# Row maxima go by one transfer from an SBUF strip into the query stacks, and the instruction order is planned anew with other delays

## The chip, the core and the metric

The kernel runs on one core of one Trainium2 chip. The metric is the device time of one execution in microseconds; lower is better. Kernel times are medians of several runs, and the profile is one further execution with the hardware profiler on. The engines are TensorE (PE; PEld is its weight load), VectorE (DVE), ScalarE (ACT), GpSimd (POOL) and SyncE (SP), which issues nearly all DMA transfers. Each engine takes its instructions strictly in program order and waits on semaphores for the others.

## The reference

A sequence of 2048 tokens of width 640 goes through two attentions of 32 heads of 20 columns, and a sigmoid gate per token mixes them (in short):

```python
g = sigmoid((x * gate_w).sum(-1, keepdims=True))
return g * A(x) + (1 - g) * B(x)

# A: four segments of 512 tokens
logits = q_s @ k_s.T * scale + mask              # causal within the segment
o = sig(beta) * (phi(q_s) @ M) / (phi(q_s) @ z + 1e-6) + (1 - sig(beta)) * softmax(logits) @ v_s
M = M + phi(k_s).T @ v_s;  z = z + phi(k_s).sum()  # phi(t) = t + 1 if t > 0 else exp(t)
# B: causal, window of 256 tokens
softmax(where(mask, q @ k.T * scale, -1e9)) @ v
# each with its own projections wq, wk, wv (wqkv) and wo
```

All is float32. The projections run in TensorE's float32r format; to keep the precision, their operands are split into a high half and a low half (the rest), and three products are added.

## The kernel before

The work is cut into 16 stages T (four segments times four groups of 16 heads; `head(T)` gives the group, in the order 0, 2, 1, 3, and the segment; groups 0 and 1 are attention A, 2 and 3 are B) and each stage into 4 units, so 64 units u of one segment, four heads at a time and two row halves r of TensorE. A unit takes about 15 us. Per stage TensorE makes the q and k projections (`gemm2`, L547) and the v projection (`v_mm`, L688); their weights and x chunks are split into halves by ScalarE (`copy`, L485) and by `split_l` (L501), which GpSimd or VectorE runs. A tiny copy named tick (L485 or L487) hands a PSUM bank from one row half to the other. The projections are stored to DRAM (`qk_store`, L591 and L593; `phi_store`, L615) and read back, rearranged, into one of four query stacks `qks` in SBUF (`stack_read`, L761, and for attention B L766 for q and L764 for k). So unit u + 4 uses the stack of unit u again.

Attention needs every row's maximum before the exponentials:

1. `max_mm` (L790): TensorE multiplies q and k, 16 matmuls a unit, into a PSUM bank per row half; `max_red` (L800): VectorE adds the mask and takes the row maximum, 16 times a unit, into `mx`, 128 x 16.
2. `max_high`, `max_low` (L804 ScalarE, L808 GpSimd) split the maxima into two halves in `mrs`, 128 x 32; `max_turn` (L812, VectorE) transposes it in blocks of 32 x 32 into `mt`, 128 x 32.
3. `max_store` (L816, SyncE) writes `mt` to DRAM (`dmx`), in an order that makes rows of 512 queries; `max_rows` (L820, SyncE), twice a unit, reads two rows of 1024 back into partitions 60 and 61 (and 124 and 125) of the query stack.
4. `st_mm` (L844): TensorE multiplies k and q again, with the two extra rows, so that the maximum is taken off inside the matmul; ScalarE takes the exponential into `P` (`st_exp`, L851), GpSimd cuts the diagonal (L857, L860), and TensorE multiplies by v (`av_mm`, L876). VectorE and GpSimd transpose, divide and transpose back (L947, L956, L974, L979, L983, L987), and the result goes by DRAM to the output projection (L547 with `ohl`, at the very end L539).

The order of instructions is not written out by hand. Each step is given to `Plan.add` with a due time in units, the engine (or two engines, "pool|dve", of which the planner takes one), a length and what it reads and writes. `Plan.order` then plays the engines: at each step it takes, among the items whose inputs are ready, the one that can start first (within TO or TP), by the shifted due time, and puts it at the end of its engine's program. The lags between engines in that play are FROM_PE, TO_PE (XP) and OTHER (XO), a transfer lands after its issue, its packets' time and DM. Due times come from constants: a stack is read at u - RD, the maxima stand at u - MT + i MQ, the steps of the maxima at u - MS; a table SHIFT moves each kind of step by an amount for each stage. DP is a handicap of VectorE where it and another engine could take an item.

Of the kernel before, what the change touches and what calls it, by code (L numbers as in the profile page):

```python
# [20 lines left out]
DH = 20  # L21
S = 2048
L = 512
# [15 lines left out]
NXS, NWS, NH, CAP = 4, 2, 1, 7  # L39
TP, TO, GP = 0.003, 0.0247, -0.9848  # L40
SW, SX, EV, WX, WS = 0.0838, 1.1218, 0.4057, 2, 1
AHEAD, RD, PACE = 6.0079, 2.1812, 3.8108
TA, TB, TC, WL = 3.9765, 0.2, 0.6, 0.0166
P0, MA, DP, NF, NR = 4.4219, 0.7417, 0.1294, 1, 1
MQ = 0.059
MT, MS = 1.677, 0.6472
WARM = 26
LM, LR, LA, AT = 0.6542, 1.1233, 0.108, 0.1204
DM, DS, SV, XP, XO, XS = 1.2, 0.35, 1.2, 0.2, 0.15, 0.04
# [3 lines left out]
ML, MN, QF, XT, OC, PL = -0.4052, -0.1569, 0.789, 0.0334, 0.1092, -0.6407  # L53
FE = -17
BACK, BULK, FT, FL = 3.3992, -1.1875, 1.0, 63
EPS = 1e-6
KINDS = dict(v_mm="v", max_mm="x", st_mm="s", tiled_mm="t", mem_add="a", split_h="h", split_l="l", m_high="e", m_low="e", v_out="e",
# [3 lines left out]
    a=(0.906, 0.762, 0.711, 0.288, -0.209, -3.157, -0.759, -0.444, 2.687, -1.073, -0.036, -1.619, 0.786, -0.987, 0.501, -1.076, 1.313, -0.983),  # L61
    c=(0.731, -0.093, -0.385, -0.167, -0.708, 0.703, 0.113, -0.061, 0.619, -0.11, -1.531, 0.072, -0.295, 0.055, -0.214, 0.043, -0.116, 0.411),
    d=(0.746, 0.239, 0.185, -0.082, 0.39, -0.063, 0.049, 0.317, -0.528, -0.276, -0.057, 0.559, -0.263, -1.344, -0.501, -0.266, 0.361, 1.353),
    e=(-4.249, 1.705, -0.128, 1.795, -1.311, 0.375, 0.842, -0.859, -0.461, 0.272, 0.494, -0.544, -0.178, -0.287, 2.233, 0.044, -2.89, 1.8),
    h=(3.212, -2.663, 1.644, 0.274, -0.301, 0.013, 0.501, -0.114, -0.071, -0.293, 0.303, 0.463, -0.151, 0.762, -0.002, -0.347, 0.662, -0.328),
    k=(-1.744, -0.243, 1.033, 0.232, -1.993, -0.368, -0.02, -0.301, -1.273, 0.311, -0.255, -1.133, -1.234, -0.63, 0.61, -0.279, -0.896, -0.594),
    l=(-0.219, -0.343, 4.432, 0.781, -0.987, 1.191, 0.933, -0.293, -0.21, 1.28, -0.466, 0.015, 1.949, -0.379, 0.201, 0.427, -0.789, -0.258),
    m=(-0.194, -1.25, -0.559, 0.371, -0.176, -0.004, 0.425, -0.115, 0.656, -0.29, -0.044, 0.247, 0.485, 0.245, 0.058, 0.06, 1.813, -2.594),
    o=(0.447, 0.881, 0.107, 0.382, 0.356, 0.191, -0.067, -0.696, 0.079, 0.169, 0.62, 0.011, -0.183, 0.133, 0.283, 0.535, -0.544, -0.683),
    p=(-1.445, -1.34, 2.498, -0.474, 0.624, 2.786, -1.141, -0.742, -0.084, -1.343, 0.092, -0.609, 0.968, 2.279, 0.395, 2.302, 0.043, -1.228),  # L70
    q=(-2.546, 0.691, 1.246, -0.428, 0.638, -0.221, -0.402, 0.036, -1.863, -1.785, 0.296, 0.473, 0.706, 0.742, -2.897, 0.134, 0.48, 1.045),
    r=(-1.009, -0.59, -0.055, 0.287, -0.49, -0.014, -0.236, 0.411, -0.328, 0.404, -0.154, -0.199, 0.678, -0.837, 1.105, -0.417, 0.238, 0.648),
    s=(-0.013, 0.309, -0.873, -0.733, 0.119, 0.011, 0.192, -0.467, -0.129, 0.092, -0.213, -1.611, -0.06, -0.193, -0.209, -0.054, -0.151, -0.401),
# [298 lines left out]
def attention(ctx, tc, const, dram, xt, wqk, wv, wo, beta, o_dram, out):  # L372
# [94 lines left out]
    def pair(w):  # L467

        return max(0.108, w * 0.000449 + 0.001)
# [333 lines left out]
    def max_high(u):  # L803
        nc.scalar.activation(mrs[u % 2][:, 0:16], B["M", u], AF.Copy)  # L804
# [483 lines left out]
```

## Time and profile before

| | |
|---|---|
| Median of 3 runs | 1002.24 us (997.16 to 1002.91) |
| Profiled execution, own time | 998.83 us |
| its span, first to last instruction | 997.1 us |
| mean granted TensorE clock | 0.994 |
| TensorE busy | 980.8 us, 98% |
| VectorE busy | 759.8 us, 76%, 2638 instructions |
| ScalarE busy | 666.9 us, 67%, 1601 instructions |
| GpSimd busy | 635.1 us, 64%, 862 instructions |
| DMA queue | 246.62 MB, 79.1% of 16 engines' span |

In the page and the views, a row such as "L790 <- DMA qks<-dkb: 3.9, 1, 3.9" of the waits is: who waited, for whom, us in all, times, longest. A row of the groups ends in busy us, mean ns of one, and the idle time just before them with what ended it. A row of the chain or of a timeline starts with its start and its length in us. A row of the windows has the stretch, its length, then the busy time of PE, PEld, DVE, ACT and POOL, the granted clock, the DMA share and GB/s. SPq is SyncE's queue, where a row's length is that of issuing a transfer. TensorE's busy share says that some matmul was under way; two row halves run at once, so a busy TensorE may still run one half alone.

### The profile page before, as it was taken

Reading aid. Unit: us, or ns where it says so; the run is one execution under the profiler, and the core shown is the slowest. Engines: PE = TensorE matmul, PEld = TensorE weight load, DVE = VectorE, ACT = ScalarE, POOL = GpSimd, SP = SyncE. Lnnn points to the kernel's source line nnn. Section 1 sums busy time; section 2 is a strip of 40 time slices with the busy share of each in tenths; the row PEclk is TensorE's granted clock in tenths of the full one; section 3 lists DMA queues with packets and bytes.
Section 4 is the critical chain, followed back from the end, with each engine's and each line's share of the span. In section 5 each row is a group of like instructions: output and inputs, shape, how many; then the busy total and the mean of one; then the engine's idle time right before and its main releaser. Section 6 shows DMA issues by size and latency. Waiting matters only on the chain.

```text
span 997.1 us, 30570 instructions
## 1 busy us (share of the span) xinstructions
PE 980.8 (98%) x11295; PEld 823.4 (83%) x11295; DVE 759.8 (76%) x2638; ACT 666.9 (67%) x1601; POOL 635.1 (64%) x862
## 2 busy tenths in 40 slices
PE   8999999999999899999999999999999999999998
PEld 7998888788878798888988898798888888877776
DVE  3279888888888586887867888679777886788944
ACT  4437767878577585776867676586677766755671
POOL 4335466847575496766966478585786666955650
PEclk9999999999999899999999999999999999999999
DMA  8899898889987879789798787969977898486433
GB/s 279 275 307 280 277 275 287 241 271 277 285 253 221 280 220 298 244 262 288 237 272 277 232 273 218 272 195 311 316 224 232 242 299 270 146 262 204 169 97 101
DMA packets 158037, 248.57 MB, mean 249 GB/s; under 512 B 52032, under 2 KB 68288, under 8 KB 157888
## 3 DMA queue, kind: packets, MB, share of 16 engines
q1 hardware_dynamic: 157888, 246.62, 79.1%
q8 instruction: 89, 1.46, 0.6%
q14 instruction: 60, 0.49, 0.2%
HBM read 150.88 MB, written 95.68 MB: 247 GB/s over the span
## 4 chain that ended last, share of the span: by engine, by line
PE 87%; DMA 5%; DVE 4%; SPq 1%; ACT 1%; POOL 1%; issue 1%; DVEq 0%; ACTq 0%
PE bank L547 40%; PE bank L688 15%; PE bank L876 14%; PE bank L790 8%; PE bank L844 8%; DMA wst<-wqk 3%; DVE bank L800 2%; PE bank L539 1%; PE bank L903 1%; DMA qks<-dkb 1%; DMA wvs<-wv 1%; PE bank L923 1%; DMA out<-ys 1%; POOL w L501 1%; DVE ys L1027 0%
## 5 line engine op out<-in xcount | busy, mean ns | idle before, releaser
L851 ACT ACTIVATE P<-bank 128x512 f32<-128x512 f32 (+2 forms) x768 | 382.1, 552 | 114.9 <-PE bank L844 73.3
L547 PE MATMUL bank<-xhl,w 64*128 64x512 f32 x2400 | 454.4, 400 | 0.5 <-DVE xhl L501 0.4
L547 PEld LDWEIGHTS bank<-xhl,w 64*128 64x128 f32 x2400 | 326.3, 186 | 12.7 <-DVE xhl L501 1.1
L790 PE MATMUL bank<-qks 60*128 60x384 f32 (+3 forms) x1024 | 302.0, 334 | 5.8 <-DMA qks<-dkb 3.9
L688 PE MATMUL bank<-wv,xhl 64*128 64x320 f32 (+1 forms) x1920 | 290.5, 317 | 1.9 <-ACT wv L485 1.3
L800 DVE CUSTOM_DVE_ANT_0 bank<-bank,mask_b 128x384 f32<-128x384 f32 (+2 forms) x512 | 259.9, 555 | 30.4 <-PE bank L790 25.0
L800 DVE CUSTOM_DVE_ANT_0 bank<-bank,mask_a 128x256 f32<-128x256 f32 (+3 forms) x512 | 239.9, 513 | 40.1 <-PE bank L790 29.2
L844 PE MATMUL bank<-qks 62*128 62x384 f32 (+3 forms) x1216 | 263.6, 303 | 2.6 <-ACT P L851 1.4
L688 PEld LDWEIGHTS bank<-wv,xhl 64*128 64x128 f32 x1920 | 247.2, 188 | 6.3 <-issue 2.1
L547 PE MATMUL bank<-ohl,w 64*128 64x512 f32 x1050 | 226.3, 400 | 0.4 <-DVE tick_dve L487 0.2
L501 POOL TENSOR_TENSOR w<-wst,w 128x640 fp32r<-128x640 f32 x109 | 170.4, 1565 | 82.6 <-ACT w L485 74.5
L857 POOL TENSOR_SCALAR_AFFINE_SELECT P<-P 128x512 f32<-128x512 f32 x256 | 161.5, 638 | 89.3 <-ACT P L851 73.6
L844 PEld LDWEIGHTS bank<-qks 62*128 62x128 f32 x1216 | 197.8, 186 | 19.7 <-issue 4.5
L790 PEld LDWEIGHTS bank<-qks 60*128 60x128 f32 x1024 | 177.3, 185 | 24.3 <-issue 11.9
L876 PE MATMUL bank<-P,vau 128*32 128x384 f32 (+3 forms) x2432 | 159.9, 407 | 0.5 <-DVE mx L800 0.2
L547 PEld LDWEIGHTS bank<-ohl,w 64*128 64x128 f32 x1050 | 153.4, 185 | 6.7 <-issue 0.8
L800 DVE DVE_READ_ACCUMULATOR2_ANT mx<- 128x1 f32 x1024 | 145.7, 142 | 0.0
L876 PEld LDWEIGHTS bank<-P,vau 128*32 128x32 f32 x2432 | 69.4, 109 | 78.2 <-issue 62.8
L485 ACT ACTIVATE w<-wst 128x640 fp32r<-128x640 f32 x121 | 89.2, 738 | 36.8 <-DMA wst<-wqk 18.6
L947 DVE STREAM_TRANSPOSE ot<-bank 128x512 f32<-128x512 f32 x64 | 45.7, 715 | 69.9 <-PE bank L876 67.7
L860 POOL TENSOR_SCALAR_AFFINE_SELECT P<-P 128x512 f32<-128x512 f32 x112 | 71.4, 646 | 8.8 <-ACT P L851 7.7
L501 POOL TENSOR_TENSOR wv<-wvs,wv 128x322 fp32r<-128x322 f32 x80 | 66.3, 845 | 11.4 <-ACT wv L485 11.0
(74 smaller groups left out, 791.7 us busy)
## 6 DMA issues: line engine op xcount, KB each, us to landing
qks<-dqk SPq DMA_DIRECT2D x32, 1024.0 KB
wst<-wqk SPq DMA_DIRECT2D x80, 320.0 KB
qks<-dkb SPq DMA_DIRECT2D x24, 768.0 KB
qks<-dqb SPq DMA_DIRECT2D x32, 512.0 KB
o_dram<-ot SPq DMA_DIRECT2D x64, 256.0 KB
wst<-wo SPq DMA_DIRECT2D x41, 320.0 KB
wvs<-wv SPq DMA_DIRECT2D x16, 805.0 KB
xst<-o_dram SPq DMA_DIRECT2D x35, 256.0 KB
```

The lines of the kernel that those rows point to most:

```text
L485: nc.scalar.activation(dst, src, AF.Copy)
L501: EN[e].tensor_tensor(out=t[:, 1], in0=B.pop(src), in1=f(t[:, 0]), op=ALU.subtract)
L547: nc.tensor.matmul(B[key], B[wkey][64 * r:64 * r + 64, a, 128 * c:128 * c + 128], B[xkey, c][64 * r:64 * r + 64, b], start=start, stop=sto ...
L688: nc.tensor.matmul(B["v", T, b][:, :n], B[("x", s), c][64 * r:64 * r + 64, a, 128 * b:128 * b + 128], B["wv", T, c][64 * r:64 * r + 64, bb ...
L790: nc.tensor.matmul(psum(("mx", u, p, b, r))[:, :n], fr(q), keys(u, 3 * DH, r, p, c0, n), start=True, stop=True)
L800: nc.vector.tensor_tensor_reduce(out=x, in0=x, in1=mk, scale=1.0, scalar=BIG, op0=ALU.add, op1=ALU.max, accum_out=B["M", u][:, j:j + 1])
L844: nc.tensor.matmul(B[k][:, c:c + 128 * n], keys(u, K, r, p, WIN + 128 * kb, 128), fr(q[64 * r:64 * r + K, L * p + 128 * q0:L * p + 128 * ( ...
L851: nc.scalar.activation(B["P", u, b][:, 2 * r + p, c0:c1], B["st", u, b, p, r][:, c0:c1], AF.Exp, scale=SCALE)
L857: nc.gpsimd.affine_select(out=v, in_=v, pattern=[[0, 4], [1, 128]], compare_op=ALU.is_ge, fill=0.0, base=0, channel_multiplier=-1)
L860: nc.gpsimd.affine_select(out=v, in_=v, pattern=[[0, 4], [-1, 128]], compare_op=ALU.is_gt, fill=0.0, base=0, channel_multiplier=1)
L876: nc.tensor.matmul(o[32 * j:32 * j + 32, 128 * q0:128 * (q0 + n)], v[:, VA * h:VA * h + 32], t[:, j, c:c + 128 * n], start=(b == 0 and i = ...
L947: nc.vector.transpose(t, B["o", u])
```

## The change

The maxima's two halves are laid out per row half in `mrs` (same sizes). `max_turn` is now four transposes of 32 x 32 that put the four blocks side by side into a strip `mt` of 32 partitions x 128. `max_store` and its DRAM tile are gone; `max_rows`, still twice a unit on SyncE, copies 16 partitions of the strip straight into two partitions of the query stack, in packets of 512 bytes. In the planner the lengths and lags are other (FROM_PE now FP), as are nearly all constants and the whole table SHIFT, so every engine's order is new. In the changed file most lines stand one further down than before (L547 is L548, L844 is L845); `max_turn` is L818 and `max_rows` L823.

```diff
-NXS, NWS, NH, CAP = 4, 2, 1, 7
+NXS, NWS, NH, CAP = 4, 2, 1, 6
-AHEAD, RD, PACE = 6.0079, 2.1812, 3.8108
+AHEAD, RD, PACE = 6.0079, 2.3371, 4.108
-P0, MA, DP, NF, NR = 4.4219, 0.7417, 0.1294, 1, 1
-MQ = 0.059
-MT, MS = 1.677, 0.6472
+P0, MA, DP, NF, NR = 4.126, 0.8297, -0.009, 1, 1
+MQ = 0.0912
+MT, MS = 1.5923, 0.7487
-DM, DS, SV, XP, XO, XS = 1.2, 0.35, 1.2, 0.2, 0.15, 0.04
+DM, DS, SV, XP, XO, XS = 1.8786, 0.35, 1.2, 0.2932, 0.2024, 0.04
+FP = 0.1682
...
-    d=(0.746, 0.239, 0.185, -0.082, 0.39, -0.063, 0.049, 0.317, -0.528, -0.276, -0.057, 0.559, -0.263, -1.344, -0.501, -0.266, 0.361, 1.353),
+    d=(-2.103, 0.036, 0.308, 0.665, 0.758, 0.476, 0.293, 0.05, -0.356, 0.199, -0.347, -0.96, 0.409, 0.244, -0.145, 2.489, -1.553, -1.487),
...
-    FROM_PE, TO_PE, OTHER = 0.25, XP, XO
+    FROM_PE, TO_PE, OTHER = FP, XP, XO
...
     def max_high(u):
-        nc.scalar.activation(mrs[u % 2][:, 0:16], B["M", u], AF.Copy)
+        nc.scalar.activation(parts(u)[:, :, 0], B["M", u].rearrange("p (r c) -> p r c", r=2), AF.Copy)
...
+    def parts(u):
+
+        return mrs[u % 2].rearrange("p (r h c) -> p r h c", r=2, h=2)
 
     def max_turn(u):
-        t = B["mt", u] = work.tile([128, 32], F32, name="mt", tag="mt")
-        nc.vector.transpose(t, f(mrs[u % 2]))
-
-    def max_store(u):
-        d = B["dmx", u] = dram.tile([2, 4, L], F32, name="dmx", tag="dmx", bufs=3)
-        nc.sync.dma_start(bass.AP(tensor=d.tensor, offset=d.offset, ap=[[32, 4], [128, 32], [1, 32]]), B["mt", u])
+        t = B["mt", u] = work.tile([32, 128], F32, name="mt", tag="mt")
+        for i in range(4):
+            nc.vector.transpose(t[:, 32 * i:32 * i + 32], f(mrs[u % 2][32 * i:32 * i + 32]))
 
     def max_rows(u, r):
-        d = B["dmx", u]
-        nc.sync.dma_start(qks[u % NQ][64 * r + 3 * DH:64 * r + 3 * DH + 2, 0:2 * L], bass.AP(
-            tensor=d.tensor, offset=d.offset + 2 * L * r, ap=[[4 * L, 2], [1, 2 * L]]))
-
+
+        at = 64 * r + 3 * DH
+        nc.sync.dma_start(qks[u % NQ][at:at + 2, 0:2 * L], B["mt", u][16 * r:16 * r + 16])
...
-        add(t + .01, DVE, 0.12, max_turn, u, get=[("mr", u)], new=[("mt", 2, ("mt", u))])
-        add(t + .03, SP, DJ, max_store, u, get=[("mt", u)], size=16384, packet=128, rings=4, new=[("dmx", 3, ("dmx", u))])
+        add(t + .01, DVE, 0.3, max_turn, u, get=[("mr", u)], new=[("mt", 2, ("mt", u))])
         for r in range(2):
-            add(t + .04 + .001 * r, SP, DJ, max_rows, u, r, get=[("dmx", u)], put=[("qr", u)], size=8192, packet=4096, rings=2)
+            add(t + .03 + .001 * r, SP, DI, max_rows, u, r, get=[("mt", u)], put=[("qr", u)], size=8192, packet=512)
```

How the order moves is shown at three places.

First place: SyncE's program where unit 22's stack is read, before. The stacks are qks_88 to qks_91 for units 0 to 3, 4 to 7 and so on, so qks_90 is unit 22's; dqb_109 and dkb_111 are the DRAM tiles of its q and k, dqk_108 the one that the next stage's projections are stored to, dphi_114 takes the phi rows of a stage of attention A.

```order
L591 DMA dqk_108<-ml 64x512
L593 DMA dqk_108<-ml 96x2x512
L591 DMA dqk_108<-ml 96x512
L593 DMA dqk_108<-ml 32x2x512
L591 DMA dqk_108<-ml 32x512
L820 DMA qks_88<-dmx 2x1024 x2
L615 DMA dphi_114<-phi 16x4x512
L766 DMA qks_90<-dqb_109 128x1024
L764 DMA qks_90<-dkb_111 128x2x768
```

The same place now, where L767 and L765 are the reads and L823 the writes of the maxima:

```order
L891 DMA qfs_106<-dphi_113 20x2x256 x8
L519 DMA wvs<-wv 128x5x322
L767 DMA qks_90<-dqb_109 128x1024
L823 DMA qks_91<-mt 2x8x128 x2
L993 DMA o_dram_62<-ot 128x512
L494 DMA wst<-wqk 128x640
L765 DMA qks_90<-dkb_111 128x2x768
L594 DMA dqk_108<-ml 128x2x512
```

Unit 22's two reads stood behind the next stage's stores; they now stand ahead of the first of them.

Second place: SyncE's program where unit 23's stack (qks_91) is read, before:

```order
L493 DMA wst<-wqk 128x640
L816 DMA dmx<-mt 4x32x32
L766 DMA qks_91<-dqb_109 128x1024
L764 DMA qks_91<-dkb_111 128x2x768
L518 DMA wvs<-wv 128x5x322
```

and now, the rows up to the second read:

```order
L592 DMA dqk_108<-ml 96x512
L594 DMA dqk_108<-ml 32x2x512
L592 DMA dqk_108<-ml 32x512
L616 DMA dphi_114<-phi 16x4x512 x2
L494 DMA wst<-wqk 128x640
L765 DMA qks_91<-dkb_111 128x2x768
```

The two reads stood together; now the second is apart from the first, behind the next stage's stores.

Third place: the start of VectorE's program, before. wv_237 to wv_280 are the tiles of the first v weights, xhl are chunks of x, w are projection weights, gh is a small constant; each TENSOR_TENSOR is the making of a low half.

```order
L417 TENSOR_SCALAR gh<-gh 128x8
L418 RECIPROCAL gh<-gh 128x8
L419 TENSOR_SCALAR gh<-gh 128x8
L501 TENSOR_TENSOR xhl<-xst,xhl 128x512
L501 TENSOR_TENSOR w<-wst,w 128x640
L487 COPY tick_dve<-bank 1x1 x3
```

and now:

```order
L420 TENSOR_SCALAR gh<-gh 128x8
L502 TENSOR_TENSOR wv_237<-wvs,wv_237 128x322
L502 TENSOR_TENSOR wv_240<-wvs,wv_240 128x322
L502 TENSOR_TENSOR wv_243<-wvs,wv_243 128x322
L502 TENSOR_TENSOR xhl<-xst,xhl 128x512
L502 TENSOR_TENSOR wv_258<-wvs,wv_258 128x322
L502 TENSOR_TENSOR w<-wst,w 128x640
```

Four of the five low halves of the first v weights, which stood on GpSimd, now stand on VectorE around the last chunk of x.

More of the change, by code (lines that the diff above doesn't have):

```diff
@@ L65 @@
[L65 to L72, printed above, removed]
@@ L467, in pair @@
     def pair(w):
-        return max(0.108, w * 0.000449 + 0.001)
+        return w * 0.000449 + 0.0035
     def unit(u):
@@ L640, in plan_pair @@
                     c, i = divmod(n, 3)
-                    add(t0 + n * dt / 3, PEH[r], 0.231, gemm2, k, wkey, x, r, c, i, ph == n == 0, ph == 1 and n == 3 * NC - 1,
+                    add(t0 + n * dt / 3, PEH[r], 0.2333, gemm2, k, wkey, x, r, c, i, ph == n == 0, ph == 1 and n == 3 * NC - 1,
                         bank=("pj", NPP, k) if ph == n == 0 else (), mod=[k] if ph or n else [],
```

44 lines of the change are left out of this document (26 added, 18 removed).

## The prediction

> **What bounds the kernel now.** I read the page's engine list first, then the chain that ended last, then what the TensorE queue itself waited for.
>
> ```profile
> span 997.1 us, 30570 instructions
> ...
> PE 980.8 (98%) x11295; PEld 823.4 (83%) x11295; DVE 759.8 (76%) x2638; ACT 666.9 (67%) x1601; POOL 635.1 (64%) x862
> ...
> PE 87%; DMA 5%; DVE 4%; SPq 1%; ACT 1%; POOL 1%; issue 1%; DVEq 0%; ACTq 0%
> ```
>
> ```profile
> PE bank L790 <- DMA qks<-dkb: 3.9, 1, 3.9
> ```
>
> TensorE holds 98% of the span and 87% of the chain. The changed program has the same matmuls, line by line and shape by shape (1024 maxima, 1216 scores, 3450 of L547, 1920 of L688 and so on), so the term of PE's own work is 0, and at most the 13% of the chain that is not PE, 130 us, can move. The rows of the PE queue's own waits show one long one: 3.9 us for a stack read, unit 22's. SyncE's timeline, the chain, TensorE's timeline and the windows around it say how it came about:
>
> ```profile
> 322.17 0.57 SPq L820 DMA_DIRECT2D qks<-dmx  x2
> 322.79 0.54 SPq L615 DMA_DIRECT2D dphi<-phi  x1
> 323.43 0.54 SPq L766 DMA_DIRECT2D qks<-dqb  x1
> 324.01 0.45 SPq L764 DMA_DIRECT2D qks<-dkb  x1
> ```
>
> ```profile
> 324.01 7.41 DMA qks<-dkb
> ```
>
> ```profile
> 326.89 0.69 PE L547 MATMUL bank<-xhl,w 64*128 64x512 f32 x4
> 331.52 0.69 PE L790 MATMUL bank<-qks 60*128 60x384 f32 x2 [3.94 <-DMA qks<-dkb]
> ```
>
> ```profile
> 325.00:330.00 5.00, 2.58 (x36) 1.75 (x20) 1.66 (x4) 2.67 (x7) 3.06 (x5) 1.00 0.92 301
> 330.00:335.00 5.00, 3.48 (x22) 3.51 (x24) 1.96 (x7) 1.11 (x3) 2.70 (x4) 0.53 1.01 349
> 335.00:340.00 5.00, 5.00 (x45) 4.90 (x44) 3.66 (x12) 3.77 (x9) 1.11 (x3) 0.78 0.80 279
> ```
>
> SyncE was issuing one transfer after another, and the read came out only at 324.01, landing 7.41 us later while the DMA engines were busy 0.92 to 1.01. TensorE stood for 3.94 us and then ran at 0.53 and 0.78 of its clock: 3.48 x (1 - 0.53) + 5.00 x (1 - 0.78) = 2.7 us more. The stall costs 3.9 + 2.7 = 6.6 us.
>
> **The change, part by part.** *The stack reads.* This is the first place of the order shown with the change. Unit 22's read stood behind the stores of the next stage and now stands ahead of all of them. Between the last score matmul of unit 18, which frees the stack, and unit 22's first maximum the program now has 215 matmuls instead of 170; 980.8 us over the program's 9503 matmuls (some run as two of the trace's 11295) is 0.103 each, so 45 are 4.6 us more room, beside a stall of 3.9. Term: -6.6, between 0 (rival B) and -6.6.
>
> *The start.* The subtractions that make the low halves of the first v weights (wv) leave GpSimd (the third place shown). Three of the five now stand ahead of the last x chunk and a fourth right behind it; the fifth stays on GpSimd. In GpSimd's timeline and the chain:
>
> ```profile
> 12.07 5.00 POOL L501 TENSOR_TENSOR wv<-wvs,wv 128x322 fp32r<-128x322 f32 x5 [7.33 <-ACT wv L485]
> ```
>
> ```profile
> 13.00 3.97 PE bank L688 x24
> ...
> 590.72 0.84 PE bank L688 x10
> ```
>
> GpSimd makes one a microsecond, and 24 matmuls that wait for them take 3.97 us where later ones take 0.084 each, 2.0. So up to 2.0 us can go; I take -1.5.
>
> *VectorE's load.* The one transpose of 128 x 32 becomes four of 32 x 32, and the lists of VectorE's instructions show what else has come over from GpSimd and ScalarE: ticks 20 to 96, v evictions (L487 vau) 18 to 27, low halves of w 12 to 32, of wv 0 to 24, of xhl 5 to 11, of ohl 5 to 17, output products (L979) 2 to 13 and sums 0 to 3.
>
> ```profile
> L812 DVE STREAM_TRANSPOSE mt<-mrs 128x32 f32<-128x32 f32 x64 | 13.0, 204 | 11.4 <-POOL mrs L808 11.1
> L501 DVE TENSOR_TENSOR w<-wst,w 128x640 fp32r<-128x640 f32 x12 | 11.7, 977 | 12.9 <-ACT w L485 12.8
> L487 DVE COPY vau<-bank 128x320 f32<-128x320 f32 x18 | 8.7, 484 | 3.8 <-PE bank L688 3.7
> ...
> L501 DVE TENSOR_TENSOR ohl<-xst,ohl 128x512 fp32r<-128x512 f32 x5 | 3.4, 719 | 2.9 <-ACT ohl L485 2.9
> L487 DVE COPY tick_dve<-bank 1x1 f32<-1x1 f32 x20 | 2.9, 143 | 13.2 <-PE bank L547 4.7 <-PE bank L688 4.4 <-PE bank L844 3.6
> ...
> L979 DVE TENSOR_TENSOR ot<-ot,den 128x320 f32<-128x320 f32 x2 | 1.0, 492 | 0.7 <-POOL den L974 0.7
> ```
>
> ```profile
> L501 POOL TENSOR_TENSOR w<-wst,w 128x640 fp32r<-128x640 f32 x109 | 170.4, 1565 | 82.6 <-ACT w L485 74.5 <-DMA wst<-wqk 3.6 <-ACT tick_act L485 3.2
> ...
> L501 POOL TENSOR_TENSOR wv<-wvs,wv 128x322 fp32r<-128x322 f32 x80 | 66.3, 845 | 11.4 <-ACT wv L485 11.0
> ```
>
> Ticks 76 x 0.143 = 10.9, evictions 9 x 0.484 = 4.4, w 20 x 0.977 = 19.5, wv 24 x 0.53 (0.977 scaled as GpSimd's 845 to 1565) = 12.7, xhl and ohl, of one shape, 18 x 0.719 = 12.9, products and sums 14 x 0.492 = 6.9: 67 us. No 32 x 32 transpose is in the trace. One that costs a quarter of a 128 x 32 adds nothing (four are 0.204), one that costs as much adds 192 x 0.204 = 39. Back to back on VectorE:
>
> ```profile
> 117.33 0.21 DVE L935 STREAM_TRANSPOSE macc<-mraw 128x32 f32<-128x32 f32 x1
> 117.47 0.21 DVE L956 RECIPROCAL den<-ot 128x16 f32<-128x16 f32 x1
> ```
>
> The next instruction starts 0.14 us after a transpose of 32 columns; the columns per partition are the same here, so I take 192 x 0.14 = 27. VectorE goes from 759.8 to about 854 us. The Trainium skill, in "VectorE: DVE Perf Modes", section "The DRAIN you can't avoid", says that a VectorE instruction does not start until the one before has left the pipe, so that the count of instructions is what to keep low; by it the four would cost 0.204 each, the 39, and the trace's 0.14 beside a length of 0.21 disagrees. VectorE's idle time covers this where there is any:
>
> ```profile
> 60.00:300.00 240.00, 238.96 (x2917) 201.28 (x2916) 209.77 (x799) 171.98 (x441) 145.90 (x204) 1.00 0.89 275
> ```
>
> The third busy time of the row is VectorE's, 209.8 of 240, and x 854 / 759.8 it is 235.8: it still fits, barely. GpSimd is relieved of 20 x 1.565 + 24 x 0.845 = 52 us in w and wv alone, and such a half comes 0.6 us sooner from VectorE. I charge +2, between 0 and rival C.
>
> *The maxima's way.* The store L816 and its landing go; the two row writes now wait at SyncE for VectorE's transpose directly, as the store did. Behind them stand stack reads, stores and weight loads, as before.
>
> ```profile
> L816 SPq DMA_DIRECT2D dmx<-mt x64: 525/561/1016, 70.7 to 949.7; - x64
> ```
>
> ```profile
> 70.68 0.59 SPq L816 DMA_DIRECT2D dmx<-mt  x1
> ...
> 74.33 1.20 SPq L820 DMA_DIRECT2D qks<-dmx  x2
> ```
>
> ```profile
> 445.42 2.81 DMA qks<-dmx
> ```
>
> In the lines of the store, SyncE's timeline and the chain: SyncE is rid of 64 x 0.561 = 36 us of issuing. The row writes can come 3.65 us sooner (74.33 - 70.68). The order spends that: between a unit's last maximum and its first score there now stand 114 matmuls in the median, 161 before, that is 4.8 us less. No wait of PE names dmx, and on the chain it stands once with 2.81 us. Term: between 0 and -2.8, taken -1.5 with what earlier loads give. ACT's and GpSimd's halves of the maxima keep their size and number: 0, hidden as before.
>
> **The sum.** -6.6 - 1.5 + 2 - 1.5 = -7.6 against the profiled execution's own 998.83 us (span 997.1 and 1.7 around it): 991.2. The profiled run lies 3.4 us under the median of 1002.24, inside the runs' 997.16 to 1002.91, so 991 is 0.8% under the one and 1.1% under the other; I take a change within 1% as no change, about what can be told here. Case A with its own range (stall between -3.9 and -6.6, start and maxima at either end, VectorE 0 to +8): 987 to 1003.
>
> **The rivals.**
>
> *B, the stall moves on.* Unit 23's second read now stands behind the stores that unit 22's stood behind (the second place shown). If its landing is as late as 7.41 us, TensorE stands at unit 23 for the same 6.6: 991.2 + 6.6 = 998. Against it: between unit 19's last score and unit 23's first maximum 212 matmuls now, 178 before.
>
> *C, VectorE becomes the bound, slower.* A maximum holds its PSUM bank until VectorE has reduced it, one bank a row half, so late reductions stop L790. If VectorE's 30.2 us of idle at 60 to 300 (240 - 209.8) are needed as they are, because it waits there for TensorE's maxima, the stretch takes 235.8 + 30.2 = 266.0: 991.2 - 2 + 26.0 = 1015. It decides from the point where about half of that idle cannot be filled (12 us more than A, where it comes out slower than before). For it: this stretch runs with VectorE at 87% already. Against: over the whole span it still has 997 - 854 = 143 us idle.
>
> *D, the direct rows land late.* If they wait on their rings as the stack read did, 7.41 us, a unit's maxima need 1.9 from L804 to SyncE (68.8 to 70.7 in the first unit), 0.4 for three more transposes, 7.4 and half of the 1.2 that the pair of writes takes to issue, 10.3 us and the last reduction, some 100 matmuls. In the program 20 units have fewer between their last maximum and their first score, by 1.5 us in the mean: 991.2 + 20 x 1.5 = 1021.
>
> ```profile
> L804 ACT ACTIVATE mrs<-mx x64: 197/216/306, 68.8 to 949.0; 128x16 fp32r<-128x16 f32 x64
> ```
>
> In the Trainium skill, "DMA: Bandwidth & Descriptors", section "Why a DMA increments its semaphore by 16 and not by 1" has a transfer spread over the largest number of engines up to 16 that divides the outer sizes of both sides; with two partitions to write that would be two engines, which speaks for D, and no row of the trace shows the engines of one transfer. Against D: 2.81 us for the old rows on the chain.
>
> *T, the whole order is tighter.* If a tenth of the chain's 130 us outside PE goes besides: 991.2 - 13 = 978.
>
> **How the numbers follow.** A 0.50, of it 0.34 under 992 (1% under the median) and 0.16 within 1%; T 0.14; B 0.20; C 0.11 (0.09 slower, 0.02 half paid); D 0.05. Faster 0.34 + 0.14 = 0.48, same 0.16 + 0.20 + 0.02 = 0.38, slower 0.09 + 0.05 = 0.14. The range goes from T's 978 to 1007, where no stall is saved and VectorE costs 8 (998.8 + 8), and leaves out C and D, 0.16, and a little of T.
>
> **What would show it.** Right: no PE wait for qks<-dkb near 320 to 345 and a clock of 1.00 there; VectorE at 840 to 865 us busy with no long PE wait on it; a transpose near 0.14 apart; the first 24 v matmuls (L689 now) in about 2 us. Wrong: a PE wait for dkb one unit later (B), VectorE over 97% at 60 to 300 with a longer stretch (C), PE or PEld waiting for qks<-mt (D).

## The result, and the profile after

The changed kernel takes 1010.98 us in the median of four runs (1009.82 to 1012.69), the kernel before 1001.41 beside it; the ratio is 1.0104, with a 95% interval of 1.0068 to 1.0139. It is slower, by about 1%. The forecast was 991, with a range up to 1007.

The page of the changed kernel (span; busy time by engine; shares of the chain that ended last):

```profile
span 1008.1 us, 30672 instructions
...
PE 992.1 (98%) x11295; PEld 818.1 (81%) x11295; DVE 853.4 (85%) x2991; ACT 660.4 (66%) x1516; POOL 558.1 (55%) x786
...
PE 82%; DVE 10%; DMA 4%; issue 2%; SPq 1%; ACT 1%; POOL 0%; DVEq 0%; ACTq 0%; POOLq 0%
```

VectorE's share of the chain went from 4% to 10%, and its busy time is the forecast 854 to within 1 us. TensorE's idle time did not change (16.3 us of the span before, 16.0 now); its busy time rose from 980.8 to 992.1 us with the same 11295 matmuls. So the loss lies in stretches in which TensorE counts as busy and gets less done, and the page's busy shares do not show it. The stall at unit 22 is gone. In the windows of the changed kernel (columns as before: stretch, length, PE, PEld, DVE, ACT, POOL, clock, DMA share) the clock is 1.00 throughout, and the longest of TensorE's own waits for a stack read is 0.5 us:

```profile
325.00:330.00 5.00, 5.00 (x69) 2.76 (x66) 4.12 (x14) 1.84 (x4) 2.58 (x3) 1.00 0.84 259
330.00:335.00 5.00, 5.00 (x50) 4.75 (x49) 4.92 (x16) 4.95 (x13) 2.27 (x5) 1.00 0.99 344
335.00:340.00 5.00, 5.00 (x53) 4.63 (x52) 4.90 (x21) 3.59 (x9) 5.00 (x8) 1.00 0.86 251
```

```profile
PE bank L791 <- DMA qks<-dqk: 0.5, 1, 0.5
```

What is new stands in the waits of TensorE and its weight load for the reductions of the maxima (`mx`, written at L801, L800 before). First the changed kernel, then the kernel before:

```profile
PEld bank L791 <- DVE mx L801: 8.7, 26, 1.3
PEld bank L845 <- DVE mx L801: 7.2, 22, 0.7
PEld bank L877 <- DVE mx L801: 2.8, 8, 0.5
PE bank L791 <- DVE mx L801: 1.9, 6, 0.9
```

```profile
PEld bank L790 <- DVE mx L800: 2.2, 9, 0.4
PEld bank L844 <- DVE mx L800: 1.5, 5, 0.4
PEld bank L876 <- DVE mx L800: 1.5, 4, 0.4
```

Summed over all such rows of PE and PEld, 20 waits of 5.7 us have become 72 of 23.3. None is long: the one 4 us stall was replaced by many of 0.3 us. (PE and PEld can wait at the same moment, so the sum is a measure, not a loss of time.) The timeline of the changed kernel at one place where TensorE waits for VectorE behind the transposes (here the wait is put down to a tick, so it isn't in the sum):

```profile
104.88 0.83 DVE L818 STREAM_TRANSPOSE mt<-mrs 32x32 f32<-32x32 f32 x4
...
105.75 0.57 DVE L801 CUSTOM_DVE_ANT_0 bank<-bank,mask_b 128x384 f32<-128x384 f32 x1
106.23 0.14 DVE L801 DVE_READ_ACCUMULATOR2_ANT mx<- 128x1 f32 x1
106.23 0.14 DVE L488 COPY tick_dve<-bank 1x1 f32<-1x1 f32 x1
...
106.43 0.33 PE L791 MATMUL bank<-qks 60*128 60x128 f32 x2 [0.39 <-DVE tick_dve L488]
```

Four transposes hold VectorE for 0.83 us; the reduction, the tick and TensorE's next maxima stand behind them. The groups of VectorE's instructions and the issues of the row writes, in the changed kernel and (last row) before:

```profile
L818 DVE STREAM_TRANSPOSE mt<-mrs 32x32 f32<-32x32 f32 x256 | 50.7, 198 | 6.7 <-POOL mrs L809 4.0
...
L502 DVE TENSOR_TENSOR w<-wst,w 128x640 fp32r<-128x640 f32 x32 | 28.3, 885 | 26.0 <-ACT w L486 25.8
L502 DVE TENSOR_TENSOR wv<-wvs,wv 128x322 fp32r<-128x322 f32 x24 | 15.2, 665 | 0.6 <-ACT wv L486 0.6
```

```profile
L823 SPq DMA_DIRECT2D qks<-mt x128: 610/638/1147, 69.1 to 963.0; - x128
```

```profile
L820 SPq DMA_DIRECT2D qks<-dmx x128: 233/260/896, 74.3 to 955.7; - x128
```

A 32 x 32 transpose takes 0.198 us, what a 128 x 32 takes (0.204). And SyncE is not relieved: the stores are gone, but the median row write went from 0.260 to 0.638 us (the three numbers of a row are shortest, median and longest, in ns). Summed over all their issues in the traces, stores and rows took SyncE 79.8 us before, and the rows alone take 83.7 now.

### The profile page after: what moved, and what is told of

The parts are those of the page before. It is cut to its first block, busy times and chain, and to the rows that moved or that the text cites. A ratio compares the mean times of both kernels' runs of the same rounds, so it can differ in the third digit from the quotient of the medians.

```text
span 1008.1 us, 30672 instructions
## 1 busy us (share of the span) xinstructions
PE 992.1 (98%) x11295; PEld 818.1 (81%) x11295; DVE 853.4 (85%) x2991; ACT 660.4 (66%) x1516; POOL 558.1 (55%) x786
## 4 chain that ended last, share of the span: by engine, by line
PE 82%; DVE 10%; DMA 4%; issue 2%; SPq 1%; ACT 1%; POOL 0%; DVEq 0%; ACTq 0%; POOLq 0%
PE bank L548 38%; PE bank L877 13%; PE bank L689 13%; PE bank L791 8%; PE bank L845 7%; DVE bank L801 5%; PE bank L540 1%; DMA wst<-wqk 1%; PE bank L904 1%; DVE mt L818 1%; DMA qks<-dqk 1%; DVE mx L801 1%; DMA wvs<-wv 1%; PE bank L924 1%; DVE ys L1028 1%
## 5 line engine op out<-in xcount | busy, mean ns | idle before, releaser
L548 PE MATMUL bank<-xhl,w 64*128 64x512 f32 x2400 | 438.1, 399 | 1.4 <-DVE tick_dve L488 0.6
L548 PEld LDWEIGHTS bank<-xhl,w 64*128 64x128 f32 x2400 | 319.4, 186 | 13.8 <-issue 1.9
L801 DVE CUSTOM_DVE_ANT_0 bank<-bank,mask_b 128x384 f32<-128x384 f32 (+2 forms) x512 | 259.1, 552 | 13.5 <-PE bank L791 9.0
L845 PE MATMUL bank<-qks 62*128 62x384 f32 (+3 forms) x1216 | 259.5, 305 | 2.4 <-DVE ml L562 1.4
L689 PE MATMUL bank<-wv,xhl 64*128 64x320 f32 (+1 forms) x1920 | 257.8, 315 | 1.6 <-ACT wv L486 1.4
L801 DVE CUSTOM_DVE_ANT_0 bank<-bank,mask_a 128x512 f32<-128x512 f32 (+3 forms) x512 | 238.3, 511 | 17.2 <-PE bank L791 11.4
L689 PEld LDWEIGHTS bank<-wv,xhl 64*128 64x128 f32 x1920 | 224.3, 187 | 5.2 <-ACT wv L486 1.8
L548 PE MATMUL bank<-ohl,w 64*128 64x512 f32 x1050 | 227.3, 403 | 0.6 <-DVE tick_dve L488 0.5
L845 PEld LDWEIGHTS bank<-qks 62*128 62x128 f32 x1216 | 190.7, 185 | 24.6 <-DVE mx L801 7.2
L502 POOL TENSOR_TENSOR w<-wst,w 128x640 fp32r<-128x640 f32 x89 | 139.3, 1566 | 63.5 <-ACT w L486 59.2
L548 PEld LDWEIGHTS bank<-ohl,w 64*128 64x128 f32 x1050 | 151.7, 186 | 9.9 <-issue 2.9
L801 DVE DVE_READ_ACCUMULATOR2_ANT mx<- 128x1 f32 x1024 | 141.6, 138 | 0.0
L502 POOL TENSOR_TENSOR wv<-wvs,wv 128x322 fp32r<-128x322 f32 x56 | 47.7, 861 | 32.5 <-ACT wv L486 22.2
```

The costliest lines, as they stand in the source:

```text
L502: EN[e].tensor_tensor(out=t[:, 1], in0=B.pop(src), in1=f(t[:, 0]), op=ALU.subtract)
L548: nc.tensor.matmul(B[key], B[wkey][64 * r:64 * r + 64, a, 128 * c:128 * c + 128], B[xkey, c][64 * r:64 * r + 64, b], start=start, stop=sto ...
L689: nc.tensor.matmul(B["v", T, b][:, :n], B[("x", s), c][64 * r:64 * r + 64, a, 128 * b:128 * b + 128], B["wv", T, c][64 * r:64 * r + 64, bb ...
L801: nc.vector.tensor_tensor_reduce(out=x, in0=x, in1=mk, scale=1.0, scalar=BIG, op0=ALU.add, op1=ALU.max, accum_out=B["M", u][:, j:j + 1])
L845: nc.tensor.matmul(B[k][:, c:c + 128 * n], keys(u, K, r, p, WIN + 128 * kb, 128), fr(q[64 * r:64 * r + K, L * p + 128 * q0:L * p + 128 * ( ...
```

## The experiments

Times below are ratios to the kernel before, measured beside each run, with the 95% interval in brackets; 0.001 is 1 us. "Old order" is the order of the kernel before, "new order" that of the changed one. Where only what a step emits is changed, the order of the rest stays instruction by instruction.

### Path or order

*The old order with the new path.* Four transposes, no store, direct rows, emitted where the old plan has them:

```
     def max_store(u):
-        d = B["dmx", u] = dram.tile([2, 4, L], F32, ...)
-        nc.sync.dma_start(..., B["mt", u])
+        pass          # and max_turn, max_rows as in the changed kernel
```

> The kernel before with its own order, instruction by instruction, and only the maxima's way of the changed kernel: four transposes of 32 x 32 in place of one of 128 x 32, no store, the rows written straight from mt. VectorE has the transposes' extra (192 x 0.14 = 27 us) and nothing else more. Theory W (work moved to VectorE by the new plan, 67 us, makes the change slower): 996 to 1003 beside 1001.4 before, rows up to 3.65 us sooner, VectorE busy about 787. Theory N (the new way of the maxima itself costs the time, by its transposes or by late rows): 1007 to 1013, with TensorE waiting for qks<-mt or for reductions. Theory O (the new order, not the load): 996 to 1003, like W. The stall at unit 22 of about 3.9 us should stay under all three, since its stack read keeps its place.

1.0136 (1.0090 to 1.0183): slower by as much as the whole change. VectorE is busy 798.1 us, 38.3 more than before, so 192 further transposes cost 0.199 each. Theory N holds here; the moved work isn't needed for a loss.

*The new order with the old path.* The reverse, with the store emitted ahead of the first row:

```
     def max_rows(u, r):
+        if r == 0:
+            max_store(u)
+        d = B["dmx", u]
-        nc.sync.dma_start(qks[...][at:at + 2, 0:2 * L], B["mt", u][16 * r:16 * r + 16])
+        nc.sync.dma_start(qks[...][...], bass.AP(tensor=d.tensor, ...))
```

> The changed kernel with its own order and its own engine for each step, and only the maxima's way of the kernel before: one transpose of 128 x 32, a store to DRAM, and rows read from there (the store is issued ahead of the first row). VectorE busy about 853 - 27 = 826. Theory W: 1005 to 1014, the load of the moved work is still there; the rows come some 3.65 us later in an order that leaves 114 matmuls for them, so some scores may wait besides. Theory N: 997 to 1003, since what costs the time is gone. Theory O: 1010 to 1020, since the order stays and the rows come later.

1.0818 (1.0763 to 1.0873). No theory had this. The waits of SyncE's queue and of TensorE in this run:

```profile
SPq L823 <- DMA dmx<-mt: 197.4, 64, 7.2
```

```profile
PE bank L847 <- DMA qks<-dmx: 17.4, 12, 3.5
```

SyncE stood 3.1 us a unit for the store's landing, and everything queued behind it came later. In the kernel before, other transfers stand between store and rows, and SyncE waited for that landing 13.2 us in all:

```profile
SPq L820 <- DMA dmx<-mt: 13.2, 11, 2.3
```

So the 71 us that it takes over the changed kernel are the price of the old path in this place of the queue; they do not say what the new order would lose with a better place for the store.

*VectorE's surcharge back.*

```
-P0, MA, DP, NF, NR = 4.126, 0.8297, -0.009, 1, 1
+P0, MA, DP, NF, NR = 4.126, 0.8297, 0.1294, 1, 1
```

> The changed kernel with one number of the planner set back: DP, the planner's surcharge on a step that VectorE takes where another engine could, from -0.009 to 0.1294 as before. The plan then gives VectorE 12 low halves of w, none of wv, 22 ticks, 2 output products and 6 of ohl, as before (32, 24, 96, 16 and 17 in the changed kernel); the four transposes, the direct rows and all other numbers stay. VectorE busy about 853 - 67 = 786. Theory W: the loss goes, 992 to 1003. Theory O (the other numbers of the order cost the time): 1007 to 1013 stays. Theory N: 1007 to 1013 stays as well.

1.0837 (1.0785 to 1.0890), with VectorE at 801 us. It separates nothing: the planner made another order for all engines out of that one number. From here on work was moved with the order held.

*Each transpose made twice, in the new order.*

```
-        for i in range(4):
+        for i in (0, 0, 1, 1, 2, 2, 3, 3):
```

> The changed kernel with each of its four transposes made twice, one behind the other, so 256 more on VectorE in the same order; nothing else differs. VectorE busy about 853 + 256 x 0.14 = 889. It prices VectorE's time directly. Theory W: VectorE is what ends the waits, so time follows its load: if 94 us more of it cost the 20 us that the forecast missed, 36 us more cost about 7 to 8, 1018, and up to 1047 where all of it shows. Theory O: VectorE's load does not matter, 1010 to 1013. Theory N by late rows: 256 x 0.14 / 64 = 0.56 us later per unit, at most a few us, 1011 to 1016.

1.0629 (1.0570 to 1.0689), 52 us more than the change for 256 transposes of 0.199 us, 51 us: all of their time is paid. The median, 1060 us, lies above the 1047 that was the most any theory allowed. In the waits of this run:

```profile
PEld bank L791 <- DVE mx L801: 28.7, 32, 1.8
PEld bank L845 <- DVE mx L801: 18.8, 25, 1.6
PE bank L791 <- DVE mx L801: 18.1, 23, 1.3
```

All such rows come to 84.8 us in 113 waits.

### Transposes or rows

*Old order, old path, three spare transposes a unit.*

```
         nc.vector.transpose(t, f(mrs[u % 2]))
+        for i in range(3):
+            nc.vector.transpose(spare, f(mrs[u % 2][32 * i:32 * i + 32]))
```

> The kernel before, with its way through DRAM, and three more 32 x 32 transposes into a spare tile right behind each unit's 128 x 32 one: 192 more instructions on VectorE of 0.198 us, 38 us, and nothing else. It prices the transposes by themselves in the old order, where the direct way with them took 13.6 us more than before. Theory W2 (VectorE's time is what the direct way costs): 1010 to 1018, since the stores also come 0.6 us later. Theory N2 (the direct rows land late): 998 to 1004.

1.0109 (1.0073 to 1.0144): 11 us from transposes alone (VectorE is 30.8 us busier), with the DRAM path kept and the result unchanged.

*One transpose of the four, direct rows, in either order.*

```
-        for i in range(4):
-            nc.vector.transpose(t[:, 32 * i:32 * i + 32], f(mrs[u % 2][32 * i:32 * i + 32]))
+        nc.vector.transpose(t[:, 0:32], f(mrs[u % 2][0:32]))
```

> The kernel before with its own order and direct rows from a 32 x 128 tile, but only the first of the four transposes is made; the other three quarters of the tile stay at zero, so three quarters of the maxima are left out and are taken as zero. VectorE's load is that of before, the row writes are those of the change. Theory W2: the 13.6 us of the direct way with four transposes go, 992 to 1001 beside 998 to 1001 before. Theory N2: 1008 to 1013 stays.

> The changed kernel with its own order, but only the first of the four transposes of a unit is made; the other quarters of the tile stay at zero, so three quarters of the maxima are taken as zero. VectorE busy 853 - 38 = 815. Theory W2: doubling the transposes cost 49 us for 47 of VectorE's, so 38 less give back 15 to 38, 972 to 996. Theory O (the order): 1005 to 1011.

Old order 1.0008 (0.9983 to 1.0034), new order 0.9970 (0.9945 to 0.9995). So the direct rows by themselves give nothing that can be told in the old order, and three transposes a unit cost 1.0136 - 1.0008, 12.8 us, there and 1.0104 - 0.9970, 13.4 us, in the new one, each uncertain by 4 to 5 us. That is a third of VectorE's 38 us, where the 256 further ones of the run above were paid in full: a transpose has no fixed price. With one transpose the waits for `mx` fall to 5.9 us (old order) and 6.9 us (new order), what they were before the change:

```profile
PEld bank L847 <- DVE mx L804: 2.6, 9, 0.5
...
PEld bank L879 <- DVE mx L804: 1.7, 5, 0.4
PEld bank L794 <- DVE mx L804: 1.6, 6, 0.4
```

*The moved work given back in the new order*, step by step where it stands:

```
+    def give(kind, e, other, every):
+        n = seen[kind] = seen.get(kind, -1) + (e == "dve")
+        return other if e == "dve" and n % every[0] not in every[1] else e
     def split_l(src, key, e):
+        e = give("l" + kind, e, "pool", ...)     # and in join, v_out, o_mult, o_sum
```

> The changed kernel with its own order, step by step, and the steps that came over to VectorE given back one by one where they stand: low halves of w 32 to 12, of wv 24 to 0, of xhl and ohl 28 to 13, products and sums 16 to 2 to GpSimd, ticks 96 to 20 and v evictions 27 to 18 to ScalarE. VectorE busy 853 - 55 to 70 = 783 to 798, GpSimd about 635. Theory W2 (VectorE's load): 985 to 1000. Against it theory G: in this order the halves are wanted by TensorE sooner than GpSimd makes them (1.565 for 0.885 us): 1010 to 1040, with waits of TensorE for w and wv of GpSimd.

1.0128 (1.0089 to 1.0166), with VectorE at 803.5 instead of 853.4: no gain. The waits for `mx` stay at 25.3 us, and TensorE's waits for GpSimd go from 6.1 to 12.8, as theory G has it. Theory W2 in its plain form, that VectorE's load as such is the price, falls.

### The stall, the place, and three ways out

*The stall alone.* The old order with unit 22's reads right behind the matmul that frees their stack:

```
+        at = max(i for i, x in enumerate(name) if x == ("st_mm", (18,))) + 1
+        reads = [i for i, x in enumerate(name) if x == ("stack_read", (22,))]
+        items[at:at] = [items.pop(i) for i in reversed(reads)][::-1]
```

> The kernel before with one thing moved: unit 22's two stack reads are issued right behind the last score matmul of unit 18, ahead of the stores of the next stage, as the changed kernel has them. It prices the stall alone, which the forecast put at 6.6 us (3.94 of waiting and 2.7 of slow clock). Theory S (the stall's price comes back): 992 to 995 beside 999, with no wait of TensorE for qks<-dkb near 326 to 340. Theory L (what comes behind catches up anyway, since the stages have other limits): 997 to 1000.

1.0039 (1.0010 to 1.0067): not faster, and slower than either theory had it. SyncE's, ScalarE's and TensorE's timelines of this run, and the windows behind:

```profile
314.63 0.34 SPq L771 DMA_DIRECT2D qks<-dqb  x1
315.02 0.43 SPq L769 DMA_DIRECT2D qks<-dkb  x1
```

```profile
324.36 0.60 ACT L562 ACTIVATE ml<-bank 128x512 fp32r<-128x512 f32 x1 [4.89 <-DMA dqk<-ml]
324.86 0.59 ACT L856 ACTIVATE P<-bank 128x512 f32<-128x512 f32 x1
325.33 0.14 ACT L490 ACTIVATE tick_act<-bank 1x1 f32<-1x1 f32 x1
```

```profile
325.50 0.68 PE L795 MATMUL bank<-qks 60*128 60x384 f32 x1 [4.57 <-ACT tick_act L490]
```

```profile
325.00:330.00 5.00, 4.50 (x25) 4.40 (x27) 2.83 (x8) 3.36 (x9) 0.63 (x1) 0.52 0.88 228
330.00:335.00 5.00, 5.00 (x44) 5.00 (x42) 3.66 (x14) 3.04 (x8) 4.79 (x5) 0.80 0.62 203
```

The reads go out 9 us earlier, and the stores they overtook (`dqk<-ml`) come later. ScalarE stands 4.89 us for a buffer that such a store has yet to empty; the tick behind it on ScalarE is late, and TensorE stands 4.57 us where it stood 3.94, with the clock at 0.52 and 0.80 behind it (0.53 and 0.78 before). It is rival B's mechanism, with another victim. So this run swaps one stall for another and does not price the stall alone.

*The same transposes in another place.* One transpose at the maxima, three spare ones behind each unit's `o_back`:

```
         nc.vector.transpose(v[:, 1], v[:, 0])
+        for i in range(3):
+            nc.vector.transpose(mts[0][32:64, 0:32], mts[1][32:64, 0:32])
```

> The changed kernel with one transpose of the four at the maxima (three quarters of the maxima are taken as zero, as in the run with one turn, 994.5) and three others of the same size behind each unit's last transpose of its output (L988's step), which nobody waits for but the store: VectorE's instructions are as many as in the changed kernel, 853 us, only their place differs. Theory P (the place costs: between a unit's maxima and its rows, ahead of the next reductions): 994 to 999. Theory W3 (VectorE's time costs wherever it is spent): 1007 to 1013.

1.0272 (1.0230 to 1.0315): 30 us for 38.7 us of VectorE, more than at the maxima. Theory P falls; the place between maxima and rows isn't special. Theory W3 fell short too (at most 1013 forecast): the same time of VectorE cost twice as much here. The waits for `mx` stand at 46.9 us in 105.

*Two transposes of 64 x 32 and four row writes; the ticks given back.*

```
-        for i in range(4):
-            nc.vector.transpose(t[:, 32 * i:32 * i + 32], f(mrs[u % 2][32 * i:32 * i + 32]))
+        for i in range(2):
+            nc.vector.transpose(t[:, 32 * i:32 * i + 32], f(mrs[u % 2][64 * i:64 * i + 64]))
...     # and in max_rows four row writes in place of two
```

```
     def join(key, e):
+        e = give("tick", e, "act", (5, (0,)))
```

> The changed kernel with two transposes of 64 x 32 a unit in place of four of 32 x 32, into a tile of 64 x 64, and four row writes in place of two (each row half from two groups of 16 partitions); the same result. VectorE saves 128 x 0.2 = 25 us, SyncE issues 128 more transfers of about 0.5 us, and a unit's rows come about 1 us later. By the runs so far 192 transposes cost 16.5 us, so 128 give back 11: theory W3: 999 to 1003. Theory D (the order is as tight on the rows as the run through DRAM showed, 77 us for about 4 us later): 1010 to 1030.

> The changed kernel with its own order, and of the work that came over to VectorE only the ticks given back: 76 of the 96 go to ScalarE where they stand, 11 us of VectorE's time and the 20 us that it stood there waiting for TensorE. Theory W3 (VectorE's time): 1003 to 1008. Theory K (the ticks are not what is late): 1009 to 1013.

Two turns: 1.0289 (1.0245 to 1.0332). VectorE fell to 830.6 us as meant, but the rows come later behind two more issues a unit, TensorE now waits for them (L847 for `qks<-mt`, 1.7 us in 3 waits) and its waits for ScalarE went from 11.2 us to 40.2. Ticks: 1.0114 (1.0079 to 1.0150), no change, theory K.

### The moved work, and the transposes given to GpSimd

What stayed open was the price of the moved work, and whether VectorE's time is what the transposes cost.

*One transpose and the moved work given back* is the sum of two edits above. *The moved work taken over in the old order* is the mirror of the second: every so many steps of GpSimd or ScalarE go to VectorE, and nothing else changes:

```
+    def take(kind, e, every):
+        n = seen[kind] = seen.get(kind, -1) + (e != "dve")
+        return "dve" if e != "dve" and n % every[0] in every[1] else e
```

> The changed kernel with one transpose of the four (three quarters of the maxima are taken as zero, 994.5 by itself) and the moved steps given back to GpSimd and ScalarE where they stand (1012.4 with four transposes). VectorE busy 815 - 50 = 765, as before the change. Theory W4 (VectorE's time is what is scarce, so the moved work costs as the transposes do, 0.43 us a us): 972 to 985. Theory G (the halves come later from GpSimd, and that costs as much as VectorE gains): 993 to 1000.

> The kernel before with its own order and its way through DRAM, and as many steps given over to VectorE where they stand as the changed kernel has there: w 12 to 32, wv 0 to 24, ohl and xhl 10 to 31, ticks 20 to 100, v evictions 18 to 28, products 2 to 13. VectorE busy about 760 + 60 = 820, GpSimd about 560. It prices the moved work alone in the old order. Theory W4: at the price of the transposes there (10.3 us for 38), 1012 to 1020. Theory G: 997 to 1003, since a half that comes sooner pays for it.

1.0025 (0.9988 to 1.0061) and 1.0210 (1.0136 to 1.0285). In the new order the moved work pays a little: giving it back costs 5.5 us (1.0025 beside 0.9970; the intervals just overlap). In the old order the same shares cost 21 us. So no price per microsecond of VectorE holds by itself; it depends on the order that the step stands in. Theory G's direction holds in the new order and fails in the old.

*The move across partitions on GpSimd*, then one 32 x 128 transpose on VectorE:

```
     def max_low(u):
         nc.gpsimd.tensor_tensor(...)
+        for i in range(4):
+            nc.gpsimd.tensor_copy(gathered[:, 32 * i:32 * i + 32], f(mrs[u % 2][32 * i:32 * i + 32]))
     def max_turn(u):
-        ...
+        nc.vector.transpose(turned, gathered)
```

> The changed kernel with the move across partitions taken from VectorE: behind the low halves of the maxima GpSimd copies the four blocks of 32 partitions side by side into a 32 x 128 tile (256 copies more there, about 0.2 us each, some 50 us in 64 stages), and VectorE turns it with one transpose of 32 x 128 in place of four. The result is the same, rows straight from SBUF. VectorE saves about 0.6 us a unit, 35 us. Theory W4: 995 to 1003, between the run with one turn and the change, if the copies' 0.8 us are no more than the three transposes took. Theory D (rows a bit later are dear, or GpSimd's copies push its low halves): 1005 to 1030.

> The kernel before with its own order, direct rows, and GpSimd's four copies with one transpose of 32 x 128 on VectorE. VectorE's load is that of before within some us. Theory W4: 997 to 1003, as the run with one turn (1002.0) and 10 us under the one with four (1011.5). Theory D: above 1006.

1.0106 (1.0031 to 1.0181) in the new order, 1.0205 (1.0136 to 1.0274) in the old: nothing gained over four transposes in either (1.0104 and 1.0136; in the old order the intervals overlap). The groups of GpSimd's copies and of VectorE's transpose, in the new order and then (last row) in the old:

```profile
L812 POOL COPY gathered<-mrs 32x32 f32<-32x32 f32 x256 | 53.6, 209 | 12.0
L820 DVE STREAM_TRANSPOSE turned<-gathered 32x128 f32<-32x128 f32 x64 | 19.1, 299 | 31.8 <-POOL gathered L812 31.0
```

```profile
L819 DVE STREAM_TRANSPOSE turned<-gathered 32x128 f32<-32x128 f32 x64 | 19.0, 297 | 49.7 <-POOL gathered L811 46.4 <-DMA qks<-turned 3.0
```

VectorE has 28 and 29 us less to do than with four transposes, and stands 31.8 and 49.7 us ahead of its transpose, since its queue waits in order for GpSimd. The last two runs let it go on with reductions meanwhile:

```
     def max_rows(u, r):
+        if r == 0:
+            turn_late(u)        # the transpose of max_turn
```

> The run in which GpSimd makes the move across partitions (1009.4), with VectorE's one transpose moved behind the reductions that the order has ahead of the row writes' issue, one or two in most units. In the run before it VectorE stood 31.8 us for GpSimd's copies. Theory H (what costs is the time that VectorE's queue is held between a unit's maxima and the next reductions, busy or waiting): VectorE stands there no more, 996 to 1004. Theory D (rows later by about half a us cost as much): 1008 to 1030.

> The kernel before with its own order, direct rows, GpSimd's four copies, and VectorE's one transpose where the row writes are issued, some ten steps of VectorE later than in the run above it (1018.1, where VectorE stood 49.7 us ahead of its transpose). In this order the rows had a landing more to wait for, so they have the time. Theory H: 999 to 1005, as the run with one turn (1002.0). Theory G2 (GpSimd's 51 us of copies are what costs, by its selects of P): 1012 to 1020.

1.0104 (1.0063 to 1.0144) and 1.0193 (1.0155 to 1.0231). VectorE's standing fell to 8.2 us and 1.1 us, the waits for `mx` from 20.8 to 10.3 us and from 20.7 to 15.3, and the time did not follow; theory H falls. In the new order the waits of TensorE for P of ScalarE rose from 5.7 us to 16.3, but the run with one transpose, the fastest of all, has 14.1 of them, so they don't explain the loss. That 51 to 54 us of copies on GpSimd cost about as much as 38 us of transposes on VectorE is measured; by which chain, in either order, is not settled.

No version with the full result beat the kernel before. The fastest, 0.9970, leaves out three quarters of the transposes.

## Why the prediction was wrong

The runs with one transpose allow the forecast's sum to be put beside a measured one, in us of about 1000:

| step | forecast | measured |
|---|---|---|
| the direct rows alone, VectorE's load kept (old order) | -1.5 | +0.8 (-1.7 to +3.4) |
| the new order with its moved work (stall, start, shares), 0.9970 against 1.0008 | -8.1 for stall and start | -3.8 |
| the three more transposes a unit, 1.0104 against 0.9970 | part of VectorE's +2 | +13.4 |
| sum | -7.6 | +10.4 |

The measured column adds up by construction, since its rows are differences of runs that lead from the one kernel to the other; each of the last two is uncertain by some 4 us. The second row can be split once more: the run with one transpose and the moved work given back (1.0025) says that 5.5 us of gain come from the moved work, the first v weights included, and leaves +1.7, not clear of 0, for all else in the new order. In the forecast's own terms: VectorE's load, transposes and moved work together, came to 13.4 - 5.5 = +7.9 for +2; stall, start and whatever else the new order does came to +1.7 for -8.1. Of the 18 us between -7.6 and +10.4 about 10 lie in the credit for the stall and the start and 6 in VectorE's load, and both steps failed.

**VectorE's load, +2: the first step that failed.** The three more transposes a unit alone cost 13.4 us; with what the moved work gains it is +7.9, at the very end of the forecast's 0 to +8. "It still fits, barely" and "I charge +2" took idle time of VectorE as cover. VectorE's idle between 60 and 300 us did not need to run out: it is busy 220.6 of 240 there in the changed kernel, 92%, under the 97% that the forecast named as C's sign:

```profile
60.00:300.00 240.00, 236.92 (x2853) 192.79 (x2852) 220.63 (x853) 164.65 (x416) 135.76 (x192) 1.00 0.84 264
```

The waits fit another reading: a reduction that comes 0.6 us later makes TensorE wait whether or not VectorE idles 5 us afterwards. So rival C had the right victim (late reductions stop the maxima) and the right side, but the wrong condition; it was priced as one stretch that runs full, and came as 72 short waits over the whole span. Among the runs that differ in transposes alone the time followed these waits. In the new order, against the run with one transpose, 16.4 us more of them go with 13.4 us of time, 40.0 with 30 (the other place) and 77.9 with 66 (doubled). In the old order 11.2 went with 10.9 (spare transposes, beside the kernel before) and 14.5 with 12.8 (the new path, beside one transpose). That the transposes cost the time is shown by runs; that they do it by these waits is argued from how the two go together, since no run keeps the transposes and takes the waits away. The runs on GpSimd, and the one with two transposes (16.0 us of such waits at 1.0289), show that it isn't the only way to lose.

**The 0.14 per transpose** was mis-sized: the row it came from had a transpose followed by a reciprocal, not by a transpose. Four take 0.83, and 192 more cost 38.3 us of VectorE. The Trainium skill's rule in "VectorE: DVE Perf Modes", section "The DRAIN you can't avoid", which the prediction weighed and set aside with its 39 us, is what this trace bears out for a row of transposes: each of 0.198 us starts 0.21 us behind the one before. That VectorE's 854 was met to 1 us is luck: transposes 11 too low, the moved work 12 too high (93.6 in all less 38.3 is 55.3, where 67 was forecast; by their own rows the moved steps come to about 71, and the busy time counts an overlap with a neighbour once).

**The stall, -6.6: the second step that failed.** It went, as the steps said, with the clock at 1.00. Its price did not come back with it: alone in the old order, the earlier read turned into a wait of 4.57 us for another engine, and in the new order, where it is gone, the +1.7 above holds no sign of 6.6. The forecast put everything else in the new order at nothing, so whether the stall was worth less or something else took its place stays open. The idle and slow-clock time of a stall is what can be saved at most; I wrote it as the likeliest value, with rival B only at the next unit's read.

**The start, -1.5.** The first matmuls of v did not fall to 2 us. The chain of the changed kernel still has them at 0.15 each (0.165 before, 3.97 us for 24):

```profile
12.59 2.56 PE bank L689 x17
```

In the first 50 us TensorE has run 400 matmuls where it had run 385, some 1.5 us at 0.103. That is the forecast's size, but much else differs in those 50 us, so it isn't shown to be the start's doing.

**The maxima's way, -1.5.** The rows do come sooner: from the start of a unit's transposes to the issue of its first row write the median went from 6.29 to 0.87 us in the traces. But sooner by itself gained nothing that can be told. "SyncE is rid of 36 us" left out that a row write's issue is dearer, 0.638 against 0.260 in the median, so SyncE has 3.9 us more instead. The 1.20 for a pair, taken from the first unit, was not typical: the median pair took 0.65. The row that lists all 128 issues would have hinted at it.

**D and T.** No row of TensorE's own waits in the changed kernel names `qks<-mt`, so D was rightly low; in the run with two transposes, whose rows come later, there are three such waits, 1.7 us. T's 978 was never near: even with one transpose the order gives 0.3%.

## What to carry over

When a step grows on an engine that works in order, ask who stands behind it in its queue and how soon TensorE wants that result; idle time elsewhere in the same stretch is no cover for a delay of 0.6 us, 64 times. Price a new instruction by its count, from a row in which it follows its own kind, and read issue costs from the row over all issues. And count a removed stall as a bound: test it by moving that one thing alone, since what it overtakes may become the next wait.

## What was not expected of the hardware

A transpose's time went with its columns and its count, not its partitions: 0.198 us for 32 x 32, 0.200 for 64 x 32, 0.204 for 128 x 32, 0.299 for 32 x 128. GpSimd's copy of 32 x 32 took 0.209, about as much as VectorE's transpose. Issuing a transfer into two partitions took 0.638 us in the median from 16 partitions of SBUF and 0.260 from DRAM.
